# Relative-position bias as steep sigmoids on ScalarE, one weight pair for all rows, sums combined by VectorE

## The chip, the cores and the metric

The kernel runs on one core of one Trainium2 chip. The metric is the time of one execution in microseconds on the device. The core has five engines with a queue each: TensorE (PE in the profile, PEld its weight loads), VectorE (DVE), ScalarE (ACT), GpSimd (POOL) and SyncE (SP, which here only issues transfers). Each engine takes its instructions in order; semaphores tie them together.

## The reference

Attention with a learned bias on relative position, and behind it a two-layer feed-forward block. Cut to what matters:

```python
# B, H, S, D = 4, 8, 576, 64; hidden = 32
scores = 1 / sqrt(D) * q @ k.T
psi_rel = log1p(abs(i - j))             # by distance
psi_i = log1p(max(i, 1))                # by row
x = psi_rel / psi_i
bias = maximum(x * w1 + b1, 0) @ w2     # 32 hidden units, 8 heads
attn = softmax(scores + bias)           # bias is the same for all batches
x = attn @ v                            # 2304 x 512
h = x @ w_in                            # 512 -> 2048
g = where(h >= 1, h, where(h <= -1, 0, (h + 1)**2 / 4))
out = g @ w_out
```

A hidden unit contributes where log1p(distance) * w1 > -b1 * psi_i. So the bias of a row is a sum over units of a step, 0 or 1, times two numbers: w1 * w2 * log1p(distance) / psi_i and b1 * w2.

## The kernel before, in words

There are three stages. The **bias stage** fills a table of the bias in DRAM. The **attention stage** goes through 16 pairs of heads (n in the code: two heads of one batch each), five row blocks each (k = 0 to 4): scores on TensorE, the row maximum and the bias on VectorE, exponentials on ScalarE, transposes, and the product with v. The **feed-forward stage** multiplies by w_in and w_out; its weights are loaded while it runs. Float32 operands are split into a high and a low part ("hi", "lo"; "kh", "ls"; "vs"), and the products are taken part by part.

In the bias stage the 576 rows are worked in 36 groups G of 16 rows. A group is four tiles u ("steps"), one for each four rows: partition 32 * r + c says for hidden unit c of row r at which distances the step is on. A group's rows need n = max(576 - 16 G, 16 G + 16) distances, from 576 down to 304 and up to 576 again. TensorE sums the units of a group's steps twice ("sums"): A with weights of w1 * w2 / psi_i, and B with weights of b1 * w2, each as a high and a low half in float16. Then "combine" makes t = (A + constant) * log1p(distance), bs = B * scale + constant, and y = t + bs, mirrored for the distances to the left (line 385) and straight for those to the right (line 387). SyncE stores y in DRAM (line 392), and the attention stage loads a head's rows from there (lines 484 to 490).

Who does what before the change: of a group's four steps VectorE computes three by a comparison (line 345 on a float16 copy of the distances in PSUM, line 343 in the first two groups) and ScalarE one, as a Sign (line 341). Since a Sign gives -1 and 1, that quarter's weights are halved and a constant is added later. The weights of A differ from row to row; they are made in five chunks (lines 266 to 280) by VectorE, GpSimd and ScalarE. VectorE makes t, ScalarE bs, and the two pieces of y go to GpSimd, or to VectorE where a table says so. Sums of more than 512 columns have their rest in a PSUM tile of their own (C).

Up to twelve u tiles are held, which is three groups, six tiles of t, bs and y, two of A and two of B. The splits for the first heads run inside this stage: VectorE casts k and v (lines 146, 158), GpSimd takes the remainders (line 132), and SyncE moves halves of them to other partitions (lines 173, 174). A scheduler sets the order of the instructions on each engine; where the code says keep_in_program_order, the written order stands.

Of the kernel before, what the change touches and what calls it, by code (L numbers as in the profile page):

```python
# [41 lines left out]


def by_sign(m):

    return m % 4 >= 4 - CFG["ns"][m // 4]


@with_exitstack
def attn_cpb_moe_kernel(ctx, tc, qk, vL, cb, win, wout, lw, dd, ident, ii, out):  # L50
# [86 lines left out]

    def prep(n):
# [47 lines left out]
    with ExitStack() as ph:  # L186
# [10 lines left out]
        cc = sum(CBW[:7])  # L197
# [3 lines left out]
        dd_s = up.tile([P, S], F16, tag="u", name="dd_s")  # L201
        nc.sync.dma_start(out=dd_s, in_=dd)
        w1_s, b1_s, w2_s, w8_s, w1r, b1r, w2r, m4_s, rm_s, sg_s = [cb_s[:, sum(CBW[:i]) : sum(CBW[: i + 1])] for i in range(len(CBW))]
        sg_s = sg_s.rearrange("p (a g) -> p a g", a=2)
# [28 lines left out]
        nc.vector.tensor_scalar(out=nthr, in0=m4_s, scalar1=b1_s, scalar2=None, op0=ALU.mult)  # L233
        nc.vector.tensor_scalar(out=thr, in0=nthr, scalar1=-1.0, scalar2=None, op0=ALU.mult)
# [9 lines left out]
        qf = cp.tile([P, 2, 32], F32, name="qf")  # L244
        qh = cp.tile([P, 2, 2, 32], F16, name="qh")
        nc.vector.tensor_copy(qf[:, 0, :], wf[:, 1, :])
        nc.vector.tensor_scalar(out=qf[:, 1, :], in0=wf[:, 1, :], scalar1=0.5, scalar2=None, op0=ALU.mult)
        nc.vector.tensor_copy(qh[:, :, 0, :], qf)
        nc.vector.tensor_tensor(out=qh[:, :, 1, :], in0=qf, in1=qh[:, :, 0, :], op=ALU.subtract)
        CH = CFG["ch"]  # L250
        wh = [cp.tile([P, 2, c1 - c0, 4, H], F16, name=f"wh{c0}") for c0, c1 in zip(CH, CH[1:])]
        EN = dict(p=nc.gpsimd, v=nc.vector)
        nc.vector.memset(wh[0].rearrange("p a n g h -> p (a n g h)").bitcast(F32), 0.0)
        for t, x in zip(wh[1:], CFG["ms"]):
            EN[x].memset(t.rearrange("p a n g h -> p (a n g h)").bitcast(F32), 0.0)
        wp8 = cp.tile([P, H], F32, name="wp8")
        nc.vector.tensor_scalar(out=wp8, in0=w8_s, scalar1=w1_s, scalar2=rsc, op0=ALU.mult, op1=ALU.mult)

        def weights_of(i):
            c0, c1 = CH[i : i + 2]  # L260
            n_ = c1 - c0
            f = cp.tile([P, n_, H], F32, name=f"wf{c0}")
            h = cp.tile([P, 2, n_, H], F16, name=f"wc{c0}")
            r = rm_s[:, c0:c1].unsqueeze(2).to_broadcast((P, n_, H))
            e = EN[CFG["w1"][i - 1]] if i else nc.vector
            e.tensor_tensor(out=f, in0=r, in1=wp8.unsqueeze(1).to_broadcast((P, n_, H)), op=ALU.mult)
            e = EN[CFG["wl"][i - 1]] if i else nc.vector
            if i and CFG["wcp"][i - 1] == "a":
                nc.scalar.copy(h[:, 0], f)
            else:  # L270
                nc.vector.tensor_copy(h[:, 0], f)
            e.tensor_tensor(out=h[:, 1], in0=f, in1=h[:, 0], op=ALU.subtract)
            return h

        def spread(i, h, g):
            q_ = slice(C * g, C * g + C)
            if i:
                nc.scalar.copy(wh[i][q_, :, :, g, :], h[q_])
            else:
                nc.vector.tensor_copy(wh[i][q_, :, :, g, :], h[q_])  # L280

        def weight_of(m, k):
            i = max(j for j in range(len(CH)) if CH[j] <= m)
            return wh[i][:, k, m - CH[i]].rearrange("p g h -> p (g h)")

        wc = [weights_of(0)]
        for g in range(4):
            spread(0, wc[0], g)


        ones = cp.tile([P, 1], F32, name="ones")
        nc.vector.memset(ones, 1.0)
        wf4 = cp.tile([P, 2, 4, 32], F32, name="wf4")
        nc.vector.tensor_copy(wf4, wf.unsqueeze(2).to_broadcast((P, 2, 4, 32)))
        pcs = psA.tile([P, 512], F32, tag="A", name="pcs").rearrange("p (a b) -> p a b", a=2)
        for a in range(2):
            nc.tensor.matmul(pcs[:, a, 0:1], wf4[:, a].rearrange("p a b -> p (a b)"), ones, start=True, stop=True)
        hs = cp.tile([P, 2], F32, name="hs")
        nc.vector.tensor_scalar(out=hs, in0=pcs[:, :, 0], scalar1=0.5, scalar2=None, op0=ALU.mult)
        nc.vector.tensor_tensor(out=hs[:, 1:2], in0=hs[:, 1:2], in1=s8, op=ALU.mult)  # L300
        cst = cp.tile([P, 2, NG], F32, name="cst")
        for a in range(2):
            nc.vector.tensor_scalar(out=cst[:, a, :], in0=sg_s[:, a, :], scalar1=hs[:, a : a + 1], scalar2=None, op0=ALU.mult)

        sdw = psD.tile([P, S // 2], I32, name="sd")
        sd = sdw.bitcast(F16)
        thd = cp.tile([P, S // 4], F32, name="thd")

        def distances():
            sw = cp.tile([P, 1], F32, name="sw")
            nc.vector.tensor_scalar(out=sw, in0=w1_s, scalar1=0.0, scalar2=None, op0=ALU.is_ge)
            nc.vector.tensor_scalar(out=sw, in0=sw, scalar1=2.0, scalar2=-1.0, op0=ALU.mult, op1=ALU.add)
            ra = cp.tile([P, 1], F32, name="ra")
            nc.vector.tensor_tensor(out=ra, in0=w1_s, in1=sw, op=ALU.mult)
            nc.vector.tensor_scalar(out=ra, in0=ra, scalar1=1e-30, scalar2=None, op0=ALU.max)
            nc.vector.reciprocal(out=ra, in_=ra)
            nc.vector.tensor_tensor(out=ra, in0=ra, in1=sw, op=ALU.mult)
            nc.vector.tensor_scalar(out=thd, in0=thr, scalar1=ra, scalar2=20.0, op0=ALU.mult, op1=ALU.min)  # L320
            nc.vector.tensor_scalar(out=thd, in0=thd, scalar1=-1.0, scalar2=None, op0=ALU.max)
            nc.scalar.activation(thd, thd, AF.Exp)
            nc.vector.tensor_scalar(out=thd, in0=thd, scalar1=-1.0, scalar2=sw, op0=ALU.add, op1=ALU.mult)
            nc.vector.tensor_scalar(out=dd_s, in0=dd_s, scalar1=sw, scalar2=None, op0=ALU.mult)
            nc.vector.tensor_scalar(out=sdw, in0=dd_s.bitcast(I32), scalar1=0, scalar2=None, op0=ALU.logical_shift_left)


# [6 lines left out]
        def steps(G):  # L334
            n_ = span(G)[2]
            us = []
            for sl in range(4):
                m = 4 * G + sl
                u = up.tile([P, S], F16, tag="u", name=f"u{m}")
                if by_sign(m):  # L340
                    tc.keep_in_program_order(nc.scalar.activation(u[:, :n_], lw1[:, :n_], AF.Sign, bias=nthr[:, m : m + 1]))
                elif G < CFG["fw"]:
                    nc.vector.tensor_scalar(out=u[:, :n_], in0=lw1[:, :n_], scalar1=thr[:, m : m + 1], scalar2=None, op0=ALU.is_gt)
                else:
                    nc.vector.tensor_scalar(out=u[:, :n_], in0=sd[:, :n_], scalar1=thd[:, m : m + 1], scalar2=None, op0=ALU.is_gt)
                us.append(u)
# [529 lines left out]
```

## Time and profile before

| | |
|---|---|
| three runs | 813.03, 815.49, 820.22 us (median 815.49) |
| profiled execution | 815.15 us, of it the span of the trace 813.4 us |
| busy in the span | PE 732.9, DVE 499.6, ACT 467.2, POOL 418.3 us |
| granted TensorE clock, mean | 0.960 |
| bias stage | up to some 95 us; the first bias store at 27.4, the last at 94.7 |
| HBM | 67.63 MB read, 25.12 MB written |

The profile is of one execution. Times of rows are in microseconds from the start of the span, means in nanoseconds. A duration is from start to end of an instruction; two in a row on one engine can overlap a little. "Idle before" is time in which the engine sat idle just ahead of an instruction, with what it waited for behind an arrow. The granted clock is 1.00 at 2.4 GHz and 0.50 at 1.2 GHz.

### The profile page before, as it was taken

To read this page: it belongs to the slowest core of one execution; us is meant where nothing else is said; L and a number is where in the kernel's file an instruction comes from. 1 tells how busy PE (TensorE), PEld (TensorE's weight loads), DVE (VectorE), ACT (ScalarE), POOL (GpSimd) and SP (SyncE) were. 2 spreads that over 40 slices of the span, in tenths; PEclk is the share of its full clock that TensorE was granted. 3 is DMA by queue.
4 is the path that set the end of the run, shared out by engine and by line. 5 is a ranking of instruction groups with operands and counts; after the bars stand their busy time and mean duration, and the time that the engine had idled before them with its cause. 6 is when DMAs were issued, how large, how long until landed. Compare 5 with 4: busy or idle time off the path is not lost. (4 is left out here: it accounts for less than half of the span.)

```text
span 813.4 us, 13433 instructions
## 1 busy us (share of the span) xinstructions
PE 732.9 (90%) x4692; PEld 645.8 (79%) x4692; DVE 499.6 (61%) x1021; ACT 467.2 (57%) x1014; POOL 418.3 (51%) x385
## 2 busy tenths in 40 slices
PE   2766789899989999987599989999999999999998
PEld 1232579898989989986489888999999999999996
DVE  8999868788768888866475566276322243222222
ACT  1986668788878888877398854343222233222222
POOL 5774767788766878874177744222222222222221
PEclk9967999999999999998889999999999999999999
DMA  6667787876786687435566454054000012000002
GB/s 195 181 193 207 205 197 209 234 196 176 186 247 165 165 238 175 115 106 169 178 210 206 145 176 114 1 158 134 20 1 1 1 30 77 1 1 1 1 0 79
DMA packets 58660, 103.60 MB, mean 127 GB/s; under 512 B 12496, under 2 KB 32608, under 8 KB 58592
## 3 DMA queue, kind: packets, MB, share of 16 engines
q1 hardware_dynamic: 44976, 83.08, 35.5%
q0 software_dynamic: 2304, 9.96, 6.0%
q10 hardware_dynamic: 11312, 9.70, 3.9%
q8 instruction: 37, 0.61, 0.3%
q14 instruction: 31, 0.25, 0.1%
HBM read 67.63 MB, written 25.12 MB: 114 GB/s over the span
## 5 line engine op out<-in xcount | busy, mean ns | idle before, releaser
L743 POOL TENSOR_TENSOR gl<-c,gh 128x384 fp32r<-128x384 f32 x96 | 101.9, 1061 | 247.5 <-ACT gh L742 225.0
L740 ACT ACTIVATE c<-c,half_s 128x384 f32<-128x384 f32 x96 | 59.1, 615 | 169.0 <-DVE c L739 169.0
L730 PE MATMUL h<-xh,wi 128*128 128x384 f32 x384 | 132.6, 345 | 12.3 <-DVE c L741 6.4
L739 DVE TENSOR_SCALAR c<-h 128x384 f32<-128x384 f32 x96 | 53.3, 555 | 147.2 <-PE h L732 144.2
L731 PE MATMUL h<-xl,wi 128*128 128x384 f32 x384 | 131.4, 342 | 1.0 <-POOL xl L464 0.7
L732 PE MATMUL h<-xh,wi 128*128 128x384 f32 x384 | 131.4, 342 | 0.7 <-POOL wi L119 0.7
L557 POOL TENSOR_TENSOR lo<-c,hi 128x512 fp32r<-128x512 f32 x75 | 101.9, 1363 | 58.4 <-DVE hi L556 55.9
L753 PE MATMUL y<-wo,gl 128*128 128x512 f32 x288 | 114.2, 396 | 0.0
L752 PE MATMUL y<-wo,gh 128*128 128x512 f32 x288 | 113.9, 396 | 0.0
L751 PE MATMUL y<-wo,gh 128*128 128x512 f32 x288 | 112.6, 391 | 0.0
L510 DVE CUSTOM_DVE_ANT_0 e<-S,bias 128x576 f32<-128x576 f32 x128 | 93.8, 745 | 21.1 <-PE S L508 19.9
L517 ACT ACTIVATE e<-e,mx 128x576 f32<-128x576 f32 x128 | 99.7, 780 | 4.5 <-DMA v<-in_vL_dram 1.9
L507 PE MATMUL S<-kh,qa 128*128 128x288 f32 x256 | 79.5, 326 | 18.5 <-DMA kh<-kh 6.9
L730 PEld LDWEIGHTS h<-xh,wi 128*128 128x128 f32 x384 | 73.5, 191 | 20.8 <-DVE c L741 9.9
L741 DVE TENSOR_TENSOR c<-h,c 128x384 f32<-128x384 f32 x96 | 53.3, 556 | 50.3 <-ACT c L740 50.3
L742 ACT CAST gh<-c 128x384 fp32r<-128x384 f32 x96 | 49.2, 512 | 51.2 <-DVE c L741 50.1
L731 PEld LDWEIGHTS h<-xl,wi 128*128 128x128 f32 x384 | 73.5, 191 | 6.0 <-DVE xl L466 1.3
L572 PE MATMUL T<-id_s,e 128*128 128x128 f32 x512 | 74.1, 278 | 2.6 <-ACT e L517 1.5
L732 PEld LDWEIGHTS h<-xh,wi 128*128 128x128 f32 x384 | 73.5, 191 | 1.1 <-POOL wi L119 1.1
L508 PE MATMUL S<-ls,qa 128*128 128x288 f32 x256 | 72.3, 300 | 0.0
L507 PEld LDWEIGHTS S<-kh,qa 128*128 128x128 f32 x256 | 48.6, 190 | 26.4 <-DVE mx L510 11.8
L572 PEld LDWEIGHTS T<-id_s,e 128*128 128x128 f32 x512 | 61.6, 143 | 4.3 <-ACT e L517 1.9
(141 smaller groups left out, 1557.5 us busy)
## 6 DMA issues: line engine op xcount, KB each, us to landing
bias_d<-y SPq DMA_DIRECT2D x36, 295.5 KB, 3.3
qk<-in_qk_dram SPq DMA_DIRECT2D x16, 608.0 KB
qa<-in_qk_dram POOLq DMA_DIRECT2D x16, 608.0 KB, 6.6
x<-xT SPq DMA_DIRECT2D x48, 192.0 KB, 3.4
rawi<-in_win_dram SPq DMA_DIRECT2D x16, 512.0 KB, 4.6
rawo<-in_wout_dram SPq DMA_DIRECT2D x16, 512.0 KB, 3.7
v<-in_vL_dram SPq DMA_DIRECT2D x16, 320.0 KB, 3.4
qa<-ls SPq DMA_DIRECT2D x32, 152.0 KB, 3.4
```

The lines of the kernel that those rows point to most:

```text
L507: nc.tensor.matmul(ps[:, hf, :HS], qs[:, qc], kh[:, kc : kc + HS], start=True, stop=False)
L510: nc.vector.tensor_tensor_reduce(out=ev.rearrange("p (a b) -> p a b", a=2), in0=ps[:, :, :HS], in1=bias[k][:, S * j : S * j + S].rearrange ...
L517: lambda ev=ev, j=j: nc.scalar.activation(ev, ev, AF.Exp, bias=mx[:, j : j + 1], scale=-1.0, accum_out=sm[:, 4 * j + k : 4 * j + k + 1])
L557: r = nc.gpsimd.tensor_tensor(out=lo, in0=m, in1=hi.bitcast(F32), op=ALU.subtract)
L572: nc.tensor.transpose(ps[:, tb, :], e[:, c0 : c0 + P], id_s)
L730: nc.tensor.matmul(ps[:, :TH], wh_, xh, start=k == 0, stop=False)
L731: nc.tensor.matmul(ps[:, :TH], wh_, xl, start=False, stop=False)
L732: nc.tensor.matmul(ps[:, :TH], wl_, xh, start=False, stop=k == NK - 1)
L743: nc.gpsimd.tensor_tensor(out=gl, in0=c, in1=gh.bitcast(F32), op=ALU.subtract)
L751: nc.tensor.matmul(y, gh[:, c], wo[f][0], start=f == 0, stop=False)
L752: nc.tensor.matmul(y, gh[:, c], wo[f][1], start=False, stop=False)
L753: nc.tensor.matmul(y, gl[:, c], wo[f][0], start=False, stop=f == NF - 1)
```

## The change

All of a group's steps are 0 or 1 now. Three of the four are a Sigmoid on ScalarE with a scale of 2 to the 80th, so steep that it is a step; the fourth is a comparison on GpSimd. The float16 distances, their thresholds and the set-up of both are gone. A has one pair of weights for all rows, as B has, and the division by psi_i is made where the sum is multiplied: t = A / psi_i * log1p(distance). The weights by row, their chunks, and the constants for the Sign are gone. A and B have PSUM tiles of 1024 columns, two each, so no rest is kept apart. VectorE makes t and both pieces of y, straight from PSUM: y = B * scale + t. bs is gone. One Sigmoid on a single column stands at the start of ScalarE's queue. The casts of k and v in the bias stage keep their written order. The numbers of matmul columns are the same.

```diff
-CFG = dict(ex=(9, 2, 0, 2, 9), ...
+CFG = dict(un=('paaa',) * NG, ex=(9, 2, 0, 2, 9), ...
+STEEP = 2.0**80
...
+    def early(ins):
+        if not go[0]:
+            tc.keep_in_program_order(ins)
...
-            nc.vector.tensor_copy(a["k"], a["r"])
+            early(nc.vector.tensor_copy(a["k"], a["r"]))
...
-        psC = ph.enter_context(tc.tile_pool(name="b_psC", bufs=1, space=PSUM))
-        psD = ph.enter_context(tc.tile_pool(name="b_psD", bufs=1, space=PSUM))
+        st = cp.tile([P, 1], F32, name="st")
+        tc.keep_in_program_order(nc.scalar.activation(st, half_s, AF.Sigmoid))
...
-        nc.vector.tensor_scalar(out=nthr, in0=m4_s, scalar1=b1_s, scalar2=None, op0=ALU.mult)
-        nc.vector.tensor_scalar(out=thr, in0=nthr, scalar1=-1.0, scalar2=None, op0=ALU.mult)
+        nc.vector.tensor_scalar(out=thr, in0=m4_s, scalar1=b1_s, scalar2=-1.0, op0=ALU.mult, op1=ALU.mult)
+        nc.vector.tensor_scalar(out=nthr, in0=thr, scalar1=-STEEP, scalar2=None, op0=ALU.mult)
...
-                if by_sign(m):
-                    tc.keep_in_program_order(nc.scalar.activation(u[:, :n_], lw1[:, :n_], AF.Sign, bias=nthr[:, m : m + 1]))
-                elif G < CFG["fw"]:
-                    nc.vector.tensor_scalar(out=u[:, :n_], in0=lw1[:, :n_], scalar1=thr[:, m : m + 1], scalar2=None, op0=ALU.is_gt)
+                x = CFG["un"][G][sl]
+                if x == "a":
+                    tc.keep_in_program_order(nc.scalar.activation(u[:, :n_], lw1[:, :n_], AF.Sigmoid, bias=nthr[:, m : m + 1], scale=STEEP))
                 else:
-                    nc.vector.tensor_scalar(out=u[:, :n_], in0=sd[:, :n_], scalar1=thd[:, m : m + 1], scalar2=None, op0=ALU.is_gt)
+                    EN[x].tensor_scalar(out=u[:, :n_], in0=lw1[:, :n_], scalar1=thr[:, m : m + 1], scalar2=None, op0=ALU.is_gt)
...
-            A = psA.tile([P, 512], F32, tag="A", name=f"A{G}")
-            Bp = psB.tile([P, 512], F32, tag="B", name=f"B{G}")
...
+            for a, pool_ in ((0, psA), (1, psB)):
+                ps = pool_.tile([P, 1024], F32, tag="AB"[a], name=f"{'AB'[a]}{G}")
...
-                                qh[:, 1 if by_sign(m) else 0, k, :] if a else weight_of(m, k),
+                                qh[:, a, k, :],
...
-            for ps, (c0, c1) in zip(A, pieces(n_)):
-                nc.vector.scalar_tensor_tensor(out=t[:, c0:c1], in0=ps, scalar=cst[:, 0, G : G + 1], in1=lw8[:, c0:c1], op0=ALU.add, op1=ALU.mult)
-            for ps, (c0, c1) in zip(Bp, pieces(n_)):
-                tc.keep_in_program_order(nc.scalar.activation(bs[:, c0:c1], ps, AF.Identity, scale=s8, bias=cst[:, 1, G : G + 1]))
-            e = nc.vector if G in CFG["yl"] else nc.gpsimd
-            e.tensor_tensor(out=y[:, :left], in0=t[:, left:0:-1], in1=bs[:, left:0:-1], op=ALU.add)
-            e = nc.vector if G in CFG["yr"] else nc.gpsimd
-            last_y.append(e.tensor_tensor(out=y[:, left : left + right], in0=t[:, :right], in1=bs[:, :right], op=ALU.add))
+            nc.vector.scalar_tensor_tensor(out=t[:, :n_], in0=A[:, :n_], scalar=sg_s[:, G : G + 1], in1=lw8[:, :n_], op0=ALU.mult, op1=ALU.mult)
+            for o, c in ((y[:, :left], slice(left, 0, -1)), (y[:, left : left + right], slice(0, right))):
+                last_y.append(nc.vector.scalar_tensor_tensor(out=o, in0=Bp[:, c], scalar=s8, in1=t[:, c], op0=ALU.mult, op1=ALU.add))
```

The order of three queues, as it stands before and now (the number behind a name tells a buffer; u are steps, B and C sums, bs, t and y as above).

ScalarE at the start of the bias stage, before:

```order
L238 ACT_TABLE_LOAD
L238 ACTIVATE lw_176<-lw_s,s_168 128x576
L341 ACTIVATE u_229<-lw_174,nthr 128x576
L341 ACTIVATE u_237<-lw_174,nthr 128x560
L322 ACTIVATE thd<-thd 128x144
L269 CAST wc_510<-wf_509 128x256
L278 COPY wh_188<-wc_240 32x56x8
L341 ACTIVATE u_305<-lw_174,nthr 128x544
L383 ACTIVATE bs_345<-B_250,cst,s_168 128x512
L383 ACTIVATE bs_345<-C_0_252,cst,s_168 128x64
```

The same place now (st is the single column, lw the distances' logarithms):

```order
L194 ACT_TABLE_LOAD
L194 ACTIVATE st<-half_s 128x1
L235 ACTIVATE lw_170<-lw_s,s_162 128x576
L259 ACTIVATE u_180<-lw_168,nthr 128x576
L259 ACTIVATE u_182<-lw_168,nthr 128x576
L259 ACTIVATE u_184<-lw_168,nthr 128x576
L259 ACTIVATE u_188<-lw_168,nthr 128x560
L259 ACTIVATE u_190<-lw_168,nthr 128x560
```

The steps follow one another without a break, 108 in all, up to the load of the table for the first exponential.

GpSimd around the remainders ls and vs of the first heads, before:

```order
L132 TENSOR_TENSOR ls_656<-qk_244,kh_549 128x608
L272 TENSOR_TENSOR wc_240<-wf_239,wc_240 128x224
L266 TENSOR_TENSOR wf_694<-cb_s,wp_197 128x224
L132 TENSOR_TENSOR ls_656<-qk_244,kh_549 128x608
L266 TENSOR_TENSOR wf_878<-cb_s,wp_197 128x256
L132 TENSOR_TENSOR vs_842<-v_247,vs_842 128x10x64
L385 TENSOR_TENSOR y_346<-t_344,bs_345 128x15
```

The same remainders of k now:

```order
L261 TENSOR_SCALAR u_409<-lw_168,thr 128x480
L261 TENSOR_SCALAR u_441<-lw_168,thr 128x464
L128 TENSOR_TENSOR ls_547<-qk_194,kh_449 128x608
L261 TENSOR_SCALAR u_475<-lw_168,thr 128x448
L128 TENSOR_TENSOR ls_547<-qk_194,kh_449 128x608
L261 TENSOR_SCALAR u_507<-lw_168,thr 128x432
```

The remainders used to stand ahead of all additions; now k's stand between the compares of groups 7, 8 and 9. On VectorE, where four casts stood between the second group's t and the first comparison of line 345, the cast of k that they need now stands behind the fifth group, and from the fourth group on the order is t, t and then the four pieces of y of two groups.

SyncE at the end of the bias stage, before (kh and ls with four-digit numbers are the second heads', biasL the last bias rows):

```order
L392 DMA bias_d_61<-y_1670 16x8x591
L484 DMA bias_0_2423<-bias_d_57 128x576
L485 DMA bias_0_2423<-bias_d_57 128x64
L486 DMA bias_0_2423<-bias_d_57 128x512
L490 DMA biasL_1729<-bias_d_61 64x576 x2
L173 DMA qa_112<-ls_1752 64x608
L174 DMA kh_1748<-kh_1748 64x608
L173 DMA qa_112<-ls_1752 64x608
L174 DMA kh_1748<-kh_1748 64x608
```

The same place now:

```order
L299 DMA bias_d_61<-y_1468 16x8x591
L383 DMA bias_3_1524<-bias_d_60 128x512
L173 DMA qa_112<-ls_1551 64x608
L299 DMA bias_d_61<-y_1474 16x8x591
L174 DMA kh_1547<-kh_1547 64x608
L173 DMA qa_112<-ls_1551 64x608
L387 DMA biasL_1528<-bias_d_61 64x576 x2
L174 DMA kh_1547<-kh_1547 64x608
```

Before, all four transfers of the second heads' k stood behind the load of biasL; now three stand ahead of it.

## Rows read from the trace of the kernel before

**Rows 1.** Busy time of each engine by stretch (instructions), granted clock, transfer engines' busy share, GB/s.

```profile
core 0: us, PE busy (x) PEld busy (x) DVE busy (x) ACT busy (x) POOL busy (x), PEclk, DMA share, GB/s
27.00:95.00 68.00, 43.95 (x593) 20.64 (x587) 65.92 (x150) 50.58 (x87) 45.60 (x58) 0.82 0.68 201
95.00:400.00 305.00, 277.08 (x2000) 260.40 (x1999) 238.06 (x524) 239.56 (x613) 218.06 (x182) 0.97 0.70 184
400.00:813.00 413.00, 400.65 (x1974) 360.06 (x1974) 171.51 (x278) 167.80 (x300) 137.77 (x123) 0.98 0.23 71
```

**Rows 2.** Tile bias_d: issue ns min/median/max, first and last start us.

```profile
L392 SPq DMA_DIRECT2D bias_d<-y x36: 517/518/920, 27.4 to 94.7; - x36
```

**Rows 3.** Timeline of VectorE: start us, us; first t, first score tile.

```profile
13.63 0.74 DVE L381 SCALAR_TENSOR_TENSOR t<-A,cst,lw 128x512 f32<-128x512 f32 x1
...
93.64 0.76 DVE L510 CUSTOM_DVE_ANT_0 e<-S,bias 128x576 f32<-128x576 f32 x1 [0.30 <-PE S L508]
```

**Rows 4.** Groups of 0 to 96 us: busy us, mean ns, idle before.

```profile
L345 DVE TENSOR_SCALAR u<-sd,thd 128x544 f16<-128x544 f16 (+17 forms) x102 | 39.4, 428 | 0.4 <-PE C L365 0.4
L383 ACT ACTIVATE bs<-B,cst,s 128x512 f32<-128x512 f32 (+13 forms) x36 | 25.4, 705 | 12.9 <-PE B L365 6.9 <-issue 3.3 <-POOL y L387 1.1
L381 DVE SCALAR_TENSOR_TENSOR t<-A,cst,lw 128x512 f32<-128x512 f32 (+13 forms) x36 | 23.5, 653 | 0.3
L341 ACT ACTIVATE u<-lw,nthr 128x576 f16<-128x576 f32 (+17 forms) x36 | 23.0, 652 | 0.1
L385 DVE TENSOR_TENSOR y<-t,bs 128x47 f32<-128x47 f32 (+10 forms) x11 | 9.6, 872 | 0.6 <-ACT bs L383 0.6
L238 ACT ACT_TABLE_LOAD x1 | 1.3, 1283 | 4.9 <-DMA lw_s<-in_lw_dram 4.9
```

**Rows 5.** The same by form, 0 to 100 us.

```profile
L381 DVE SCALAR_TENSOR_TENSOR t<-A,cst,lw 128x512 f32<-128x512 f32 x10 | 7.4, 740 | 0.2
L146 DVE CAST kh<-qk 128x1216 fp32r<-128x1216 f32 x2 | 1.6, 780 | 0.0
L385 DVE TENSOR_TENSOR y<-t,bs 128x271 f32<-128x271 f32 x1 | 1.1, 1077 | 0.0
L381 DVE SCALAR_TENSOR_TENSOR t<-A,cst,lw 128x304 f32<-128x304 f32 x2 | 1.0, 522 | 0.0
L341 ACT ACTIVATE u<-lw,nthr 128x576 f16<-128x576 f32 x2 | 1.5, 765 | 0.0
L341 ACT ACTIVATE u<-lw,nthr 128x560 f16<-128x560 f32 x2 | 1.5, 749 | 0.0
L132 POOL TENSOR_TENSOR ls<-qk,kh 128x608 fp32r<-128x608 f32 x4 | 6.9, 1742 | 6.8 <-DVE kh L146 6.7
L387 POOL TENSOR_TENSOR y<-t,bs 128x512 f32<-128x512 f32 x1 | 1.3, 1275 | 1.4 <-DVE t L381 1.4
L554 POOL CAST hi<-c 128x512 fp32r<-128x512 f32 x1 | 0.6, 602 | 0.0
```

**Rows 6.** Groups of the whole span, from the page: the exponentials.

```profile
L517 ACT ACTIVATE e<-e,mx 128x576 f32<-128x576 f32 x128 | 99.7, 780 | 4.5 <-DMA v<-in_vL_dram 1.9
```

**Rows 7.** Timelines of ScalarE, TensorE and VectorE: start us, us.

```profile
7.52 1.41 ACT L341 ACTIVATE u<-lw,nthr 128x576 f16<-128x576 f32 x2
...
11.96 1.05 PE L365 MATMUL A<-u,wh 128*32 128x512 f16 x8 [0.39 <-DVE wh L280]
...
23.95 0.75 DVE L381 SCALAR_TENSOR_TENSOR t<-A,cst,lw 128x512 f32<-128x512 f32 x1
24.62 0.47 DVE L345 TENSOR_SCALAR u<-sd,thd 128x512 f16<-128x512 f16 x1
```

**Rows 8.** Timeline of TensorE: the second heads' first scores.

```profile
107.80 0.37 PE L507 MATMUL S<-kh,qa 128*128 128x288 f32 x1 [3.07 <-DMA kh<-kh]
```

**Rows 9.** Transfers of 20 to 95 us.

```profile
DMA packets 7237, 14.34 MB, mean 191 GB/s; under 512 B 1341, under 2 KB 1341, under 8 KB 7228
```

**Rows 10.** As rows 1, five microseconds of the bias stage.

```profile
30.00:35.00 5.00, 2.97 (x33) 1.13 (x36) 4.61 (x9) 4.95 (x9) 1.81 (x3) 1.00 0.97 339
```

More of the change, by code (lines that the diff above doesn't have):

```diff
@@ L41, with attn_cpb_moe_kernel @@
 BIG = 3.0e38
-def by_sign(m):
-    return m % 4 >= 4 - CFG["ns"][m // 4]
+STEEP = 2.0**80
 @with_exitstack
-def attn_cpb_moe_kernel(ctx, tc, qk, vL, cb, win, wout, lw, dd, ident, ii, out):
+def attn_cpb_moe_kernel(ctx, tc, qk, vL, cb, win, wout, lw, ident, ii, out):
     nc = tc.nc
@@ L200, in attn_cpb_moe_kernel @@
         nc.sync.dma_start(out=lw_s, in_=lw)
[L201 to L204, printed above, removed]
+        w1_s, b1_s, w2_s, w1r, b1r, w2r, m4_s, sg_s = [cb_s[:, sum(CBW[:i]) : sum(CBW[: i + 1])] for i in range(len(CBW))]
         w2r = w2r.rearrange("p (c h) -> p c h", c=C)
@@ L259, in weights_of @@
[L259 to L325, printed above, removed]
@@ L329, in span @@
+        nc.vector.tensor_copy(qh[:, :, 0, :], wf)
+        nc.vector.tensor_tensor(out=qh[:, :, 1, :], in0=wf, in1=qh[:, :, 0, :], op=ALU.subtract)
+        EN = dict(p=nc.gpsimd, v=nc.vector)
         def span(G):
@@ L354, in sums @@
             n_ = span(G)[2]
-            A = psA.tile([P, 512], F32, tag="A", name=f"A{G}")
-            Bp = psB.tile([P, 512], F32, tag="B", name=f"B{G}")
-            out = [[A[:, : min(n_, 512)]], [Bp[:, : min(n_, 512)]]]
-            for a in range(2 * (n_ > 512)):
-                out[a].append(psC.tile([P, D], F32, tag=f"C{a}", name=f"C{a}_{G}")[:, : n_ - 512])
-            for a in range(2):
-                for ps, (c0, c1) in zip(out[a], pieces(n_)):
+            out = []
+            for a, pool_ in ((0, psA), (1, psB)):
+                ps = pool_.tile([P, 1024], F32, tag="AB"[a], name=f"{'AB'[a]}{G}")
+                out.append(ps)
+                for c0, c1 in pieces(n_):
                     for k in range(2):
                         for sl in range(4):
-                            m = 4 * G + sl
                             nc.tensor.matmul(
-                                ps[32 * sl : 32 * sl + 32],
-                                qh[:, 1 if by_sign(m) else 0, k, :] if a else weight_of(m, k),
+                                ps[32 * sl : 32 * sl + 32, c0:c1],
+                                qh[:, a, k, :],
                                 us[sl][:, c0:c1],
@@ L803, in attn_cpb_moe_kernel @@
         finish(0)
[L806 removed]
+_INS = ["qk", "vL", "cb", "win", "wout", "lw", "ident", "ii"]
 _OUTS = [((NT, DM), "float32")]
@@ L838, in _layout @@
     a["lw"] = np.tile(L, (P, 1))
-    a["dd"] = np.tile(pos.astype(np.float16), (P, 1))
     m4 = np.repeat(M.reshape(S // 4, 4).T, C, axis=0)
-    sign = np.array([by_sign(m) for m in range(S // 4)])
-    half = np.where(sign, f32(0.5), f32(1.0))
-    rm = np.repeat((half / M.reshape(S // 4, 4).T).astype(f32), C, axis=0)
-    on = np.repeat(sign.reshape(NG, 4).T.astype(f32), 32, axis=0)
-    sg = np.concatenate([on * np.repeat(1.0 / M.reshape(NG, 16).T, H, axis=0).astype(f32), on], axis=1)
-    w1c, b1c, w8 = np.tile(w1.reshape(C, 1), (4, 1)), np.tile(b1.reshape(C, 1), (4, 1)), np.tile(w2, (4, 1))
+    sg = np.repeat(1.0 / M.reshape(NG, 16).T, H, axis=0).astype(f32)
+    w1c, b1c = np.tile(w1.reshape(C, 1), (4, 1)), np.tile(b1.reshape(C, 1), (4, 1))
     rows = [np.tile(x.reshape(1, -1), (P, 1)) for x in (w1, b1, w2)]
-    a["cb"] = np.concatenate([w1c, b1c, w2x.reshape(P, 32), w8] + rows + [m4, rm, sg], axis=1)
+    a["cb"] = np.concatenate([w1c, b1c, w2x.reshape(P, 32)] + rows + [m4, sg], axis=1)
     eye = np.eye(D, dtype=f32)
```

30 lines of the change are left out of this document (4 added, 26 removed).

## The prediction, made before the changed kernel ran

> **What bounds the kernel now.** I read the stages first, then the bias stage's idle times and instruction prices. From 95 us on TensorE is busy 277.08 of 305 us and then 400.65 of 413, and the chain of work that ended last runs through its matmuls to the end [rows 1]. Before that, between 27 and 95 us, VectorE is busy 65.92 of 68 us while ScalarE, GpSimd and TensorE are at 50.58, 45.60 and 43.95 [rows 1]. The bias stage is bound by VectorE, everything behind it by TensorE.
>
> Two dates frame the stage. The first of 36 bias stores is issued at 27.4 us, the last at 94.7 [rows 2]; the first score tile is taken up by VectorE at 93.64 [rows 3]. So the 36 groups leave one every (94.7 - 27.4) / 35 = 1.92 us, and they begin late: VectorE has built the first weights, the distance thresholds and four casts by then.
>
> VectorE's time there goes to the steps and the sums [rows 4]: 102 compares in 39.4 us, the multiplication t in 23.5, and those y's that it takes (872 ns mean for eleven). ScalarE has 36 steps (652 ns) and the evacuation bs in 25.4 us, beside weight copies.
>
> **The change, part by part.** It alters the bias stage alone; behind the first scores the same work stands in nearly the same order. Nothing there is tied to a clock time, so what the first score tile gains is passed on, as long as transfers keep up. I therefore date that tile. A group has n columns, from 576 down to 304 and up again in steps of 16, mean 440; the two pieces of y always have 591 together.
>
> *ScalarE* loses bs and the weight copies and gets 108 steps in a row. A sigmoid is not in this trace; at 576 columns Sign takes 765 ns [rows 5] and Exp 780 [rows 6]. I price a sigmoid like Sign, the same step with the same operands. Two of them back to back, 576 and 560 wide, last 1.41 us [rows 7] where their own times are 0.765 + 0.749 [rows 5], so each start follows 0.10 earlier than the mean time says. The sum: 108 x 0.652 - 107 x 0.10 = 59.7 us. They begin where the first Sign begins, at 7.52 [rows 7], since the same two products stand ahead; the last ends at 67.2. The table for exponentials is loaded anew behind the last step; ScalarE then waits some 4 us for the first maximum, so the load's 1.28 us [rows 4] is covered; without that idle time it is added in full.
>
> *VectorE* loses 102 compares, the distance set-up and the first weights, and gets both pieces of y. t reads one operand from PSUM and one from SBUF: 740 ns at 512, 522 at 304 [rows 5], that is 1.05 ns per column and 0.20 fixed. A t started at 23.95 lasts 0.75, yet the next instruction starts at 24.62 [rows 7], so the pitch is 0.08 shorter: 0.12 + 1.05 n. Per group t takes 0.12 + 0.46 = 0.58 and y, priced likewise, 0.24 + 0.62 = 0.86: 1.45 us, 52.2 for 36. Two casts of k at 780 ns [rows 5] and one of v, half as wide, add 1.9. Its first t starts when the first group's sums are there: third sigmoid at 9.6, plus 1.67, the time from the first A matmul at 11.96 [rows 7] to the first t at 13.63 [rows 3]. VectorE alone would end at 11.3 + 54.1 = 65.4.
>
> This price of y is the weakest point. The bounds: like t, 0.86 a group, or like the y's that VectorE adds now, both operands in SBUF, at 872 ns a piece [rows 4]. One of those took 1077 ns for 271 columns [rows 5], longer than t for 304. They ran beside GpSimd's additions. I take t's price, because the new y has t's kinds of operands. The Trainium skill (SBUF — State Buffer, Who interferes with whom) says that a VectorE instruction with two SBUF inputs contends with a GpSimd instruction that reads SBUF and one with at most one SBUF input does not. By that rule y costs what t costs and the forecast stands; without it the dear y gives the second rival below. The trace's t's bear the rule out, the new y is not in it.
>
> *GpSimd* loses all its y's, the weights and three memsets, and gets 36 compares. No compare of its own is in the trace. Nearest rows: a cast at 512 columns takes 602 ns, an addition of two tiles 1275 [rows 5]. At 440 that is 0.52 or 1.10, in all 19 to 40 us; three remainders, priced at k's 1742 each, add 5.2 [rows 5]. Both ends lie under 59.7. I take 0.8, between them, but the term is hidden up to (59.7 - 5.2) / 36 = 1.51 us. In the queue the k remainders stand between the compares of groups 7, 8 and 9; they wait for a cast on VectorE. Twelve step tiles hold three groups, so some 5 us of such a wait is covered.
>
> *TensorE* has the same matmuls in the sums. Eight of 512 columns take 1.05 us at the stage's start [rows 7], so two sums of a wide group take 2.1 to 2.3, against ScalarE's 3 x 0.66 = 2.0 at 576. At the lower clock it would bind a little in the widest groups; averaged over all, 440 columns, it does not. B's two PSUM tiles are now freed by y instead of bs, so a B waits for the y two groups ahead; VectorE works t, t, y, y, and that B runs under the second y. I add 0.8 us for this and for handing over.
>
> *SyncE's queue* still issues 36 stores, each 0.52 [rows 2], against 1.66 per group. The loads of finished bias rows wait in that queue for stores to land, with later stores behind them. Six y tiles, ten us, cover that.
>
> **Sum.** Last sigmoid 67.2, its sums 1.67, t 0.72, the cast moved in front of the last y 0.70, y 0.86: 71.2, with 0.8 added 72.0, against 93.64. The gain is 21.6 us, on a profiled execution of 815.15 (span 813.4 and 1.75 around it): **793.5 us**. The three runs' median, 815.49, lies 0.3 higher. Two thirds come from the start (first store near 13 instead of 27.4), the rest from the pitch, 1.66 instead of 1.92. Own bounds: 788, if the scores' wait for k at 107.80 (3.07 us) [rows 8] goes too, since the second heads' transfers now stand mostly ahead of the last bias load; 799, if hand-overs cost 5 us more.
>
> **Rivals.**
> 1. *The transfers set the pace.* From 20 to 95 us 14.34 MB move [rows 9]; squeezed between 12.9 and 72 that asks 243 GB/s. Against it: 5 us at 339 GB/s in this stage [rows 10]. For it: such a stretch has the engines busy 0.97. If the stage's own mean of 201 GB/s [rows 1] were all, it would take 71.3 us, end at 84.2, and the time would be 805.7.
> 2. *y is dear.* With 0.79 per piece as pitch VectorE needs 2.17 a group, 78 us and 1.9 for casts: the scores start at 91.2, the time is 812.7, no change. For it speak the stretched rows named above, against it t's.
> 3. *The compare on GpSimd is not streamed.* Then every group waits for its first quarter, and GpSimd bounds the stage: 7.5 + 5.2 + 36 c + 4.0 for the tail. Above c = 1.51 it eats the gain; it is 1% slower than before from c = 2.36 on, 2.2 times the two-tile addition at 440. At three times that addition, 3.3 us, the scores start at 135 and the time is 857. Against it: every elementwise row of GpSimd lies within 2.5 ns per column; for it: none of them compares. The Trainium skill (GPSIMD Engine Reference, Performance versus the Vector engine) warns that data-dependent branching costs about 12 cycles an element, by its 1.2 GHz an estimated 4.4 us a compare and 897 us in all; its Engine selection calls one-input work roughly line rate, which would be the forecast. No run here shows either.
> 4. *The change does less than it says*: a sigmoid dearer than Sign by 0.2 us costs 21.6 and leaves 815. That Sign and Exp agree within 2% [rows 5, 6] speaks against it.
>
> **Numbers.** Forecast 0.66, most of it within 788 to 799. Transfers 0.14, mostly still faster. Dear y or dear sigmoid 0.09. Dear compare 0.07, of it 0.05 slower. Better than 788: 0.04. Within 1% (807.0 to 823.3, about what three runs can tell from no change) lie the second and fourth rivals and an edge of the first: 0.11. Faster by more 0.84, slower 0.05. The range that leaves out two in ten reaches to the first rival: 788 to 806.
>
> **What would show it.** Right: the first bias store near 13 us, the first score tile near 72; 108 steps on ScalarE at 0.65 without gaps; y at 0.2 + 1.05 per thousand columns; GpSimd's compare under 1.1 us. Transfers: SyncE's stores waiting, VectorE's y released by landed stores. Dear y: VectorE full again. Dear compare: TensorE's sums released by GpSimd. The forecast is also wrong if the scores start at 72 and the end does not follow; then a wait in the first heads, on k or on the last bias rows, is longer than now.

## The result, and the profile after

The changed kernel takes **786.66 us** (median of four runs, 785.88 to 789.02) against 815.12 for the kernel before beside it: a ratio of 0.9647, 95% interval 0.9598 to 0.9696. It is faster, and by more than forecast: 28.5 us instead of 21.6, and the time lies 1.3 us below the low end of the range. The profiled execution took 786.39 us (span 784.6).

By stretches of the span, which answers to [rows 1] (columns as there):

```profile
12.00:27.00 15.00, 10.31 (x150) 4.17 (x149) 13.51 (x26) 15.00 (x27) 13.28 (x11) 1.00 0.83 234
27.00:72.00 45.00, 34.75 (x504) 15.74 (x503) 41.62 (x87) 41.97 (x78) 37.73 (x29) 1.00 0.87 259
95.00:375.00 280.00, 254.09 (x1835) 238.77 (x1833) 220.80 (x479) 220.10 (x561) 200.28 (x166) 0.96 0.69 181
375.00:784.00 409.00, 398.94 (x1974) 358.20 (x1974) 171.30 (x277) 167.49 (x300) 139.35 (x123) 0.99 0.23 72
```

The bias stage now fills from 12 us on, and its load is spread: ScalarE is busy 15.00 of the 15 us up to 27, and then VectorE, ScalarE and GpSimd have 41.62, 41.97 and 37.73 of 45, where VectorE alone was full before. Transfers ran at 259 GB/s. Behind the stage TensorE is the bound as it was.

The issue of the bias stores, as [rows 2]:

```profile
L299 SPq DMA_DIRECT2D bias_d<-y x36: 517/532/1292, 11.7 to 71.2; - x36
```

The first store leaves 15.7 us earlier, the last 23.5: (71.2 - 11.7) / 35 = 1.70 us a group, 1.66 forecast. The two ends of the stage in the timelines of ScalarE and VectorE (start us, us), as [rows 3] and [rows 7]:

```profile
6.40 7.85 ACT L259 ACTIVATE u<-lw,nthr 128x576 f16<-128x576 f32 x12
...
9.79 0.82 DVE L292 SCALAR_TENSOR_TENSOR t<-A,cb_s,lw 128x576 f32<-128x576 f32 x1 [2.57 <-ACT u L259]
...
66.35 1.28 ACT L414 ACT_TABLE_LOAD   x1
...
67.53 0.81 DVE L292 SCALAR_TENSOR_TENSOR t<-A,cb_s,lw 128x576 f32<-128x576 f32 x1
68.25 0.79 DVE L146 CAST kh<-qk 128x1216 fp32r<-128x1216 f32 x1
68.95 0.95 DVE L294 SCALAR_TENSOR_TENSOR y<-B,s,t 128x575 f32<-128x575 f32 x2
69.82 0.75 DVE L407 CUSTOM_DVE_ANT_0 e<-S,bias 128x576 f32<-128x576 f32 x1
```

The order of the tail is the one forecast: last sigmoid, table load, t, a cast of k, y, first score tile. That tile starts at 69.82, 23.82 us earlier than in [rows 3]. The groups of the stage, 0 to 90 us (busy us, mean ns, idle before):

```profile
L259 ACT ACTIVATE u<-lw,nthr 128x576 f16<-128x576 f32 (+17 forms) x108 | 59.9, 653 | 0.0
L261 POOL TENSOR_SCALAR u<-lw,thr 128x576 f16<-128x576 f32 (+17 forms) x36 | 49.4, 1381 | 5.6 <-PE B L278 3.4 <-DVE s L225 1.7 <-PE A L278 0.4
L278 PE MATMUL A<-u,qh 128*32 128x512 f16 (+17 forms) x352 | 37.7, 330 | 19.9 <-POOL u L261 12.4 <-ACT u L259 4.5 <-DVE y L294 1.3
L294 DVE SCALAR_TENSOR_TENSOR y<-B,s,t 128x15 f32<-128x15 f32 (+35 forms) x72 | 32.9, 514 | 0.5 <-DMA bias_d<-y 0.2
L292 DVE SCALAR_TENSOR_TENSOR t<-A,cb_s,lw 128x576 f32<-128x576 f32 (+17 forms) x36 | 23.3, 666 | 7.0 <-PE A L278 4.5 <-ACT u L259 2.6
```

108 sigmoids run back to back, 59.9 us with 0.0 idle: ScalarE sets the pace, at Sign's price. GpSimd's comparison costs 1.38 us on average and stays hidden, though not by much: of the 19.9 us that TensorE waits in front of A's sums, 12.4 end with a comparison on GpSimd. That is the sign which the prediction named for a dear comparison, but it does not reach ScalarE, which waits at none of its 108 steps. VectorE still waits 7.0 us in front of its t's.

### The profile page after: what moved, and what is told of

The parts are those of the page before. It is cut to its first block, busy times and chain, and to the rows that moved or that the text cites. A ratio compares the mean times of both kernels' runs of the same rounds, so it can differ in the third digit from the quotient of the medians.

```text
span 784.6 us, 13360 instructions
## 1 busy us (share of the span) xinstructions
PE 723.6 (92%) x4688; PEld 639.3 (81%) x4688; DVE 472.2 (60%) x929; ACT 471.6 (60%) x1025; POOL 415.7 (53%) x355
## 5 line engine op out<-in xcount | busy, mean ns | idle before, releaser
L454 POOL TENSOR_TENSOR lo<-c,hi 128x512 fp32r<-128x512 f32 x75 | 100.3, 1340 | 56.5 <-DVE hi L453 53.3
L414 ACT ACTIVATE e<-e,mx 128x576 f32<-128x576 f32 x128 | 99.8, 780 | 5.3 <-DVE mx L407 3.9
```

Of the source, the lines that this page charges most:

```text
L414: lambda ev=ev, j=j: nc.scalar.activation(ev, ev, AF.Exp, bias=mx[:, j : j + 1], scale=-1.0, accum_out=sm[:, 4 * j + k : 4 * j + k + 1])
L454: r = nc.gpsimd.tensor_tensor(out=lo, in0=m, in1=hi.bitcast(F32), op=ALU.subtract)
```

## The experiments

Two questions were open. Is the stage what the forecast said it is (ScalarE its bound, GpSimd hidden below 1.51 us, the tile's date passed on one to one)? And where do the 4.9 us come from that the end gained over the tile, 815.15 - 786.39 - 23.82? Theory A: the rest is the second head's k, whose transfers now stand ahead of the last bias load. In each expectation A is the account that I held, and the rivals have letters of their own.

This table holds what the kernels are compared by: start of the first score matmul, time from there to the first feed-forward matmul, TensorE's wait for k in the first heads, median (us), and the median less the first column. The first three columns are read in the one profiled execution of each kernel, the median is over all its runs.

| kernel | first score | to feed-forward | wait for k | median | less first |
|---|---|---|---|---|---|
| before | 92.7 | 277.5 | 3.8 | 815.1 | 722.4 |
| changed | 68.4 | 274.4 | 0 | 786.7 | 718.3 |
| e5, the same again | 69.2 | 274.7 | 0 | 787.4 | 718.2 |
| e1 balanced | 68.0 | 274.2 | 0 | 788.1 | 720.1 |
| e3 4th step on VectorE | 76.7 | 274.2 | 0 | 795.7 | 719.0 |
| e4 4th step on ScalarE | 87.6 | 275.0 | 0 | 806.7 | 719.1 |
| e6 two on GpSimd | 111.5 | 277.6 | 1.3 | 829.9 | 718.4 |
| e7 old steps | 99.8 | 275.1 | 0 | 819.2 | 719.4 |
| e8 old sums | 86.4 | 277.3 | 2.5 | 808.8 | 722.4 |
| e2 k late | 69.2 | 276.7 | 1.8 | 791.8 | 722.6 |
| e12 k late, again | 69.1 | 278.2 | 2.4 | 790.8 | 721.7 |
| e10 k early | 71.3 | 274.3 | 0 | 790.2 | 718.9 |
| e9 before, k early | 97.0 | 274.5 | 0 | 815.8 | 718.8 |
| e11 before, k later | 92.9 | 277.0 | 0 | 812.5 | 719.6 |

**e3, e4: the fourth step elsewhere.**

```diff
-un=('paaa',) * NG
+un=('vaaa',) * NG      # e3
+un=('aaaa',) * NG      # e4
```

> The changed kernel with the fourth step of every group on VectorE and none on GpSimd. Theory A: ScalarE's 60 us are as before; VectorE's 56 us of products between 9.8 and 69.8 grow by 36 comparisons of about 0.55 (0.75 us at 560 to 576 columns in the kernel before, less 0.08 of overlap, at 440 columns on average), 19.8 us in all, so that VectorE bounds the stage; first score tile near 83, kernel near 800 (797 to 803). Rival E, the comparison on GpSimd (1.38 us, almost the 1.51 of a group at ScalarE's pace) holds the stage up through its hand-overs, and VectorE's has room: first score tile within 2 us of 69.8, kernel 784 to 789.

> The changed kernel with all four steps of every group on ScalarE, none on GpSimd. Theory A: 36 sigmoids of 0.55 us more, ScalarE 80 us from 6.4 on, first score tile near 89.5, kernel near 806.5, a difference to the changed kernel equal to the one of the first score tile within 1 us. Rival C, the lead of the scores isn't handed on: the kernel's difference is more than 3 us from that of the score tile. Beside it, whether GpSimd's comparisons slow VectorE's products: with none of them, t (666 ns mean) and y (514) stay within 3% if not, and get shorter by more if they do.

e3: 795.70 us (ratio to before 0.9768, 0.9735 to 0.9801), 1.3 us below the 797 to 803 of A. VectorE was the bound, as A has it (busy 63.88 of 64 us from 12 to 76), but its comparisons were cheaper than I took them, 492 ns and not 550 or more, and the tile came at 78.1, not 83. e4: 806.69 us (0.9896, 0.9871 to 0.9921), tile at 88.5: 18.7 us after the changed kernel's, for a median 20.0 later. So the bound is the engine with the longest sum, and the tile's date is passed on within 1.3 us (A had said 1, the rival more than 3). The groups of e4, 0 to 90 us:

```profile
L259 ACT ACTIVATE u<-lw,nthr 128x576 f16<-128x576 f32 (+17 forms) x144 | 79.6, 650 | 0.0
L294 DVE SCALAR_TENSOR_TENSOR y<-B,s,t 128x15 f32<-128x15 f32 (+35 forms) x72 | 34.5, 520 | 3.2
L292 DVE SCALAR_TENSOR_TENSOR t<-A,cb_s,lw 128x576 f32<-128x576 f32 (+17 forms) x36 | 24.2, 673 | 16.6 <-PE B L278 10.6 <-ACT u L259 3.6 <-PE A L278 2.3
```

With no comparison on GpSimd, t and y take 673 and 520 ns; with them 666 and 514. GpSimd's comparisons do not slow the products. The rule weighed in the prediction (the Trainium skill, SBUF — State Buffer, Who interferes with whom: a VectorE instruction with at most one SBUF input, outside the two-port modes, does not contend with GpSimd) agrees with these rows.

**e6: two comparisons on GpSimd.** The edit is `un=('ppaa',) * NG`.

> The changed kernel with two comparisons of every group on GpSimd and two sigmoids on ScalarE, to test my formula for a GpSimd that is the bound. Theory A: 72 comparisons of 1.38 us are 99.4 us from 5.8 on, with some 5 us of its other work 110; the first score tile about 3 to 4 us later, 113 to 115, the kernel near 831 (827 to 835), slower than before. Rival: the comparisons were stretched by waiting for VectorE or for step tiles and are cheaper by themselves (under 1.1 us): first score tile under 95, kernel under 812.

829.94 us, slower than before (1.0194, 1.0157 to 1.0231), tile at 112.6. The groups, 0 to 120 us:

```profile
L261 POOL TENSOR_SCALAR u<-lw,thr 128x576 f16<-128x576 f32 (+17 forms) x72 | 98.2, 1381 | 1.9 <-DVE s L225 1.9
L259 ACT ACTIVATE u<-lw,nthr 128x576 f16<-128x576 f32 (+17 forms) x72 | 41.8, 650 | 57.0 <-PE B L278 57.0
```

The price is GpSimd's own: 1381 ns again, with only 1.9 us of idle time, ScalarE now waiting 57.0 us. The third rival's mechanism is real, and with the measured price its formula comes within 4 us: 7.5 + 5.2 + 36 x 2.762 + 4.0 = 116 against 112.6. One comparison a group, at 1.38 of the 1.51 that it may cost, is 0.13 us from being the bound.

**e7, e8: one half of the change each.** e7 puts three steps back on VectorE (`un=('vvva',) * NG`). e8 has one step on VectorE and the second sum evacuated and added as before. Neither is an exact half: e7's comparisons read the float32 distances, and e8 keeps the single pair of weights and gives every addition to GpSimd.

```diff
-un=('paaa',) * NG
+un=('vaaa',) * NG
...
+            tc.keep_in_program_order(nc.scalar.activation(bs[:, :n_], Bp[:, :n_], AF.Identity, scale=s8))
-                last_y.append(nc.vector.scalar_tensor_tensor(out=o, in0=Bp[:, c], scalar=s8, in1=t[:, c], op0=ALU.mult, op1=ALU.add))
+                last_y.append(nc.gpsimd.tensor_tensor(out=o, in0=t[:, c], in1=bs[:, c], op=ALU.add))
```

> Half of the change undone: three of four steps on VectorE as before, one on ScalarE, with the new sums (one weight pair, both parts combined by VectorE from PSUM) kept. Theory A: VectorE has 108 comparisons of 0.492 us (the mean that the run with one of them showed), 53 us, beside the 56 us of products: 109 from 7.2 on, first score tile 116 to 120, kernel 833 to 837, slower than before; the new sums pay only because the steps leave VectorE. Rival: the gain comes mainly from the shorter start and the weights, and the kernel stays below 812.

> The other half undone: three of four steps on ScalarE, one on VectorE, but the second part of the sum again evacuated by ScalarE and added by GpSimd, the additions of all groups. Theory A: ScalarE has 60 us of sigmoids and 36 evacuations of some 0.63 us, 83 us from 6.4 on; GpSimd 72 additions of 0.83, 60 us; VectorE 41. First score tile 92 to 96, kernel 809 to 813, about as before: neither half of the change pays without the other. Rival: the evacuation disappears beside the sigmoids and the kernel stays below 800.

e7: 819.20 us (1.0054, 1.0034 to 1.0073). Slower than before by half a per cent, but 14 us less than I expected, with the tile at 101.2 and not at 116 to 120. The comparisons took 457 ns each and overlapped, 46.4 us in all instead of 53, and the rest overlapped too: VectorE was busy for all of the 94.0 us from 7.2 to the tile, 45.1 of them with comparisons, so that 48.9 were left for what I had put at 56. e8: 808.78 us (0.9940, 0.9913 to 0.9967), 0.2 us below the 809 to 813 expected. That is a hit on the time alone, since the tile came at 87.4 and not at 92 to 96; the profiled execution, 804.85 us, is the shortest of the four. Neither half gives more than 6 us, both together give 28: the new sums need a VectorE without the steps, and the steps need a ScalarE without the evacuation.

**e1: handing five sigmoids to VectorE.**

```diff
+un=tuple('pvaa' if g in (0, 1, 12, 24, 33) else 'paaa' for g in range(NG))
```

> The changed kernel with one of ScalarE's sigmoids handed to VectorE as a comparison in 5 of the 36 groups (0, 1, 12, 24 and 33). Theory A, the busiest engine of the stage sets the bias's end and whatever the first score tile gains reaches the end of the kernel unchanged: ScalarE loses 5 sigmoids of 0.55 to 0.64 us, some 3.0 us, VectorE gains 5 comparisons of 0.55 to 0.67, of which the first two lie in its idle 2.57 us; the first score tile moves from 69.8 to about 67, the kernel from 786.7 to about 784 (783 to 785). Rival B, VectorE (41.97 of 45 us busy in the middle of the stage) is already as much the bound as ScalarE: the first score tile stays within 0.7 us of 69.8 or comes later, the kernel 786 to 789. Rival C, the time behind the scores is not handed on (transfers or the clock set it): the first score tile moves by 3 us, the kernel by less than 1.

788.13 us (0.9668, 0.9641 to 0.9696): not faster than the changed kernel, rival B. The same stretch of the changed kernel and of e1 by windows (us, then PE, PEld, DVE, ACT, POOL):

```profile
12.00:69.00 57.00, 42.97 (x642) 18.30 (x641) 52.14 (x107) 55.58 (x101) 48.14 (x37) 1.00 0.85 256
```

```profile
12.00:68.00 56.00, 44.57 (x639) 18.58 (x631) 52.63 (x109) 52.64 (x96) 50.61 (x39) 0.94 0.85 262
```

ScalarE falls to 52.64 of 56, VectorE is at 52.63, GpSimd at 50.61: three engines are each over 90% busy, ScalarE now waits 2.0 us for B's sums, and the first score comes only 0.4 us sooner, less than the 0.8 between two executions of the changed kernel. What ScalarE loses is not gained here, with the others that near.

**e5, e2, e12, e10: what else moved.** e5 is the changed kernel again. In e2 and e12 the second head's k is prepared one row block of the attention later, which puts its transfers behind the last bias load, as before; in e10 it is prepared in group 33 of the bias stage.

```diff
-                    if t == 20 - 10 * m + i_ and 0 < n + m < N:
+                    if t + 2 * (n + m == 1 and i in (5, 6)) == 20 - 10 * m + i_ and 0 < n + m < N:   # e2, e12
...
+            if G == 33:                                # e10, e9; taken out of the attention's steps
+                for i in (1, 3, 5, 6):
+                    preps[1][i]()
```

> The changed kernel once more, unaltered, beside the others of this call. The two variants before it spread over 5 to 7 us between executions, so this tells how far the kernel's own executions spread and how much of the 28.5 us is the one execution that was profiled. If the bias stage sets the gain, the first score tile lies within 0.7 us of 69.8 again and every difference between executions behind it; the median 786 to 789. If the lead of the first profiled execution was luck, the median is 789 to 792.

> The changed kernel, with the transfers of the second head's rows (k and its low part) put behind the load of the last bias tile on SP's queue, where the kernel before had them; the bias stage is untouched. Theory A, some 2 to 3 us of the gain over my forecast is the wait for k that the new order avoids: the first score tile stays at 69.8, TensorE waits about 3 us for k near 83, the second head's sums come 1 to 3 us later than at 101.0 and the kernel takes 788.5 to 789.5. Rival D, the lead behind the bias comes from elsewhere (denser work, higher clock, chance between executions): the wait is made up for by the queued matmuls within two heads and the kernel takes 786 to 787.5.

> The changed kernel with the second head's k behind the last bias load, a second time, since its executions fell into two heaps (787.3 and 791.7 to 793). Theory A, the wait of 1.8 us and what follows from it costs some 4 us in most executions: median 790 to 792.5. Rival D, it was chance: median 786.5 to 789, as the changed kernel.

> The control: the same edit on the changed kernel, where TensorE waits for no k in the first heads. Theory A: nothing to gain, the stretch from the first score matmul to the first of the feed-forward part stays at 274 to 275.2 and the kernel at 786 to 788.5. Rival G, the early transfers help in themselves (the queue is clear for the next bias rows): the stretch under 273.5, the kernel under 785.

Over both sets the changed kernel's ten runs have a median of 787.1 us, nine of them between 785.9 and 789.1 (e5 alone: 787.41, its tile at 70.6, 0.8 us later). The thirteen runs of the late k have 791.7, eleven of them at 790.1 or more. Their bias stages are alike (first score 69.1 and 69.2 against 68.4 and 69.2), so a late k costs 4.6 us in the median. Two things stay open in this. The wait itself is 1.8 us in e2 and 2.4 in e12, less than the cost and less than the 3 us of A for e2 (788.5 to 789.5 forecast); and the profiled execution of e2, which shows the wait, is one of the two that took only 787.4 us. So what turns the wait into the cost is not shown. And the edit moves more than transfers: GpSimd begins k's low part at 77.73 us in e2 and 78.70 in e12, against 69.13 in the changed kernel. These runs test a late k, not the order of the queue by itself.

SyncE's queue, first of the kernel before, then of the changed one:

```profile
102.27 1.13 SPq L490 DMA_DIRECT2D biasL<-bias_d  x2
103.45 0.59 SPq L173 DMA_DIRECT2D qa<-ls  x1
104.08 0.60 SPq L174 DMA_DIRECT2D kh<-kh  x1
104.72 0.59 SPq L173 DMA_DIRECT2D qa<-ls  x1
105.36 0.60 SPq L174 DMA_DIRECT2D kh<-kh  x1
```

```profile
70.63 0.57 SPq L173 DMA_DIRECT2D qa<-ls  x1
71.25 0.84 SPq L299 DMA_DIRECT2D bias_d<-y  x1
72.13 0.60 SPq L174 DMA_DIRECT2D kh<-kh  x1
73.22 0.48 SPq L173 DMA_DIRECT2D qa<-ls  x1
77.12 1.31 SPq L387 DMA_DIRECT2D biasL<-bias_d  x2
78.48 0.59 SPq L174 DMA_DIRECT2D kh<-kh  x1
```

The last bias load waits for the last bias store to land: SyncE waits 4.8 us for that in the kernel before, and up to 2.2 us at once in the changed one. Before, four transfers of k were queued behind it; now three go ahead of it. TensorE's waits there (us, times, longest) in the kernel before, the changed one and e12; the second answers to [rows 8]:

```profile
PE S L507 <- DMA kh<-kh: 3.8, 2, 3.1
```

```profile
PE S L404 <- DVE mx L407: 3.0, 5, 1.0
PE S L404 <- DVE t L292: 0.9, 1, 0.9
```

```profile
PE S L404 <- DMA kh<-kh: 2.4, 2, 1.9
```

The wait is gone in the changed kernel and back in e12. e10 misses in part: its stretch is 274.3, as for A, but preparing k inside the stage delayed the first score to 71.3, and the kernel took 790.23, not 786 to 788.5.

**e9, e11: the same order in the kernel before.** e9 has the edit of e10, e11 this:

```diff
+            if G == 32:
+                with tc.issue_after(last_y[-1].ins):
+                    for i in (1, 3, 5, 6):
+                        preps[1][i]()
```

> The kernel before, with the second head's q, k and low part prepared and transferred inside the bias stage instead of behind the last bias load; nothing else is touched. So far the four variants whose k transfers stand behind that load (the kernel before among them) need 276.7 to 277.6 us from the first score matmul to the first of the feed-forward part, the six others 274.2 to 275.1. Theory A, it is this order: TensorE's 3.8 us of waiting for k near 108 go, the stretch falls to 274 to 275.2, the first score matmul stays within 0.7 us of 92.7, and the kernel takes 811 to 813 (3 us less than before). Rival F, the stretch is longer because GpSimd's additions end the bias stage late (the run with them had 277.3): it stays at 277 or more and the kernel at 814 to 816.

> The kernel before again with the second head's k prepared ahead of the last bias load, now only after the additions of group 30, so that GpSimd's 2.96 us for the low part don't hold up the stage's first groups as in the last such run (first score matmul 97.0 instead of 92.7). Theory A, the wait for k is worth 2 to 4 us in the kernel before: no wait for k in the first heads, first score matmul within 1.5 us of 92.7, the end of the second head's sums 2 us or more ahead of 128.4, kernel 811 to 813. Rival H, the last bias rows hold up the first head as long (their load was issued at 102.27 and 102.55 in both, the second sums ended at 128.39 and 128.26): the second sums stay within 1 us of 128.4 and the kernel at 814 to 816.5; the wait for k then hides another one.

e9: 815.81 us (1.0020, 0.9999 to 1.0041), no gain, against 811 to 813 forecast. The wait went and the stretch fell to 274.5, but GpSimd made k's low part amid the first groups' additions and the scores began 4.3 us later. That the time grew by only 1.0 us fits some 3 us gained behind them. The second head's row sums of the softmax were done at 128.26, as at 128.39 before. e11: 812.52 us (0.9965, 0.9933 to 0.9997), 3.1 us less than the kernel before beside it (815.65), though the interval reaches from 0.2 to 5.5 us. The scores began at 92.9 and nothing in the first heads waited for k; the second head's row sums were done at 126.63, 1.8 us sooner and not 2. But TensorE now waited 2.0 us for a row maximum of VectorE, and the stretch stayed at 277.0. So by the medians, and by e9, an earlier k is worth some 3 us in the kernel before too, if it costs the stage nothing; the profile of e11 does not show those 3 us.

The last column of the table says it in short. Where k stands ahead of the bias load, nine kernels with first scores from 68.0 to 99.8 us end 718.2 to 720.1 us later; of the five with a wait for k, four end 721.7 to 722.6 later. The exception is e6 (two runs, a wait of 1.3): 718.4. This column sets a median against the start in one execution, and within the profiled executions alone it does not part the two: with the wait they end 718.2 (e2) to 722.4 us (before) after the first score, without it 717.2 (e3) to 721.2 (e11). The stretch to the first feed-forward matmul comes from one execution each and does part them, 276.7 to 278.2 us with the wait and 274.2 to 275.1 without, save e11.

## Why the prediction was right, and where it was not

*What bounds.* Right. The bound of the stage passes from VectorE to ScalarE, and the date of the scores is passed on one to one (e3, e4, e6, e7).

*ScalarE.* 108 sigmoids at 653 ns in 59.9 us against 59.7. They began at 6.40, not 7.52; the product ahead of them (line 235; before the change, line 238) started at 5.72 instead of 6.84, which I had not allowed for.

*VectorE.* y was the weakest point and was right, 0.20 + 1.05 per thousand columns; by form, from 0 to 75 us:

```profile
L292 DVE SCALAR_TENSOR_TENSOR t<-A,cb_s,lw 128x576 f32<-128x576 f32 x2 | 1.6, 813 | 2.6 <-ACT u L259 2.6
L294 DVE SCALAR_TENSOR_TENSOR y<-B,s,t 128x576 f32<-128x576 f32 x1 | 0.8, 807 | 0.0
L294 DVE SCALAR_TENSOR_TENSOR y<-B,s,t 128x15 f32<-128x15 f32 x1 | 0.2, 231 | 0.1
```

*GpSimd.* Wrong in size and harmless. I took 0.8 us between 0.52 and 1.10; it is 1.38, above the upper bound, because no row near it was a comparison. The third rival's remark that every elementwise row of GpSimd lies within 2.5 ns a column was misread, too: the subtraction for ls in [rows 5], 1742 ns at 608 columns, is 2.87. The comparison comes to 3.14 ns a column at 440. It is not the estimated 4.4 us that the Trainium skill's 12 cycles an element would give (GPSIMD Engine Reference, Performance versus the Vector engine). Nor does it bear out that work with one input runs roughly at line rate (the Trainium skill, GPSIMD Engine Reference, Engine selection): the cast of [rows 5], with one input too, takes 1.18 ns a column. That it stayed hidden was right by 0.13 us.

*The sum* missed the profiled execution by 7.1 us, 2.2 of them up to the first score tile and 4.9 behind it. At the tile it said 72.0; the tile came at 69.82. 1.1 are the start of the sigmoids; 0.5 the last sums (66.35 to 67.53, 1.18 us, against 1.67, which was read in the kernel before's start); 0.8 the allowance for handing over, of which nothing showed, ScalarE having no idle time; the sigmoids give 0.2 back.

*What is passed on* is the step that failed: the sum put the wait for k at nothing. I took the tile's gain for the whole and left the wait for k as an outer bound at 788 with a chance of 0.04 below it, though I had written that the transfers would mostly stand ahead of the last bias load. That was visible in the order of the queues before the run and belonged in the sum: 793.5 less 3.07 gives about 790 by my own terms. In the medians of the runs it is worth 4.6 us in the changed kernel (e2, e12) and 3.1 in the kernel before (e11, 0.2 to 5.5). With 24 from the stage this makes the 28. In the profiled pair the 4.9 us behind the tile are 3.6 up to the first feed-forward matmul and 1.4 behind it, and the latter isn't explained: the feed-forward part, from its first matmul of line 627 to the last, differs between profiled executions by 5 us (426.2 in e2, 431.4 in e4).

*Rivals.* Transfers: 259 GB/s where 243 were asked, no store held up ScalarE. Dear y: no. Comparison on GpSimd: TensorE waited for it already with one of them a group, but it bound the stage only with two (e6). Dear sigmoid: no, 653 ns where Sign took 652.

## What to carry to other kernels

When a stage is shortened, look at what the new order of the queues puts ahead of its last load: a wait that goes with the reorder belongs in the sum, not at the edge of the range. An engine that is moved to must be counted with everything that it gives up: each half of this change alone is worth 6 us or less, both together 28. With three engines of a stage over 90% busy, shifting single instructions between them gave nothing more (e1).

## What the hardware showed beside that

A comparison on GpSimd (128 partitions, f32 to f16) takes 1031 ns at 304 columns and 1722 at 576, 2.54 ns a column, more than its addition of two tiles (1275 at 512 [rows 5]). From 0 to 125 us, by form, in the changed kernel:

```profile
L261 POOL TENSOR_SCALAR u<-lw,thr 128x576 f16<-128x576 f32 x2 | 3.4, 1722 | 1.7 <-DVE s L225 1.7
L261 POOL TENSOR_SCALAR u<-lw,thr 128x512 f16<-128x512 f32 x2 | 3.1, 1556 | 0.0
L261 POOL TENSOR_SCALAR u<-lw,thr 128x304 f16<-128x304 f32 x2 | 2.0, 1031 | 0.0
```

The same comparison on VectorE, 512 columns, in e3 with an almost idle GpSimd and in e8 beside GpSimd's additions:

```profile
L261 DVE TENSOR_SCALAR u<-lw,thr 128x512 f16<-128x512 f32 x2 | 1.0, 480 | 0.0
```

```profile
L261 DVE TENSOR_SCALAR u<-lw,thr 128x512 f16<-128x512 f32 x2 | 2.1, 1042 | 0.0
```

At this width it is 2.2 times as long beside them. Over all 36 the mean goes from 492 to 680 ns, and unevenly: at 560 columns it takes 506 and 538. t, with one operand from PSUM, hardly changes, 667 and 675 ns on average. So a cheap comparison on VectorE can be dear next to a busy GpSimd (in e1, beside GpSimd's comparisons, one of 560 columns took 967 ns, against 506 in e3, but one of 544 took 495 against 497). That may be a part of why e1 gained nothing; no run shows it apart.
